# A window of three loads in flight in front of an attention and token-mixing kernel

## Chip, cores, metric

The kernel runs on one core of one Trainium2 chip. The metric is the device time of one execution in microseconds. A run counts as slow when it is more than 1.5% above the fastest of the same kernel in its rounds. Ratios below are the mean time of one kernel's fast runs over that of the other's fast runs of the same rounds, so they are not quite the ratios of the medians quoted beside them. The span in a profile is about 2 us shorter than the time of the same run. The profiled run of before (145.63 us) counts as slow.

## The reference, cut to what matters

```python
# q, k, v: (8 batches, 8 heads, 576 rows, 64), float32
scores = q_c @ k_c^T / 8        # inside chunks of 64 rows
attn   = softmax(scores);  x = attn @ v          # then x as (8, 576, 512)
W      = (x @ w_q) @ (x @ w_k)^T / 8
out    = relu(W @ x) @ w_out                     # (8, 576, 512), float32
```

For each batch 3.5 MB of q, k and v (float32) have to come in. The kernel casts them to float16 on the way, so the same batch is 1728 KB in the kernel's memory.

## The kernel before

GpSimd issues every load. One batch is 12 loads: q and k for two groups of heads, each in two parts (128 and 160 KB as float16), and v in four parts (144 KB). With the weights and batch 0, which is cut a little differently, there are 99 loads.

```python
    def load_qk(b, lo, hi):
        # ... the tiles of the batch, from a pool with three buffers
        for ti in range(2):
            for hg in range(NHG):
                nc.gpsimd.dma_start(
                    qk_in[b][ti][:, hg, lo:hi, :], qk_rows[ti][b, hg][:, lo:hi, :]
                )

    def load_v(b):
        # ...
        for o in range(2):
            for r in range(2):
                nc.gpsimd.dma_start(
                    v_bufs[b % NVB][ds(o * CH + r * 32, 32), :, 0:D], src[o, r]
                )
        # ... after the last batch: issue the stores that were held back
# ...
    load_qk(0, 0, 2 * UG); make_identity(nc, ident[:]); load_v(0)
    load_qk(0, 2 * UG, NG * UG); load_w()
    load_qk(1, 0, 4); load_qk(1, 4, NG * UG); load_v(1); load_wout()
    load_qk(2, 0, 4); load_qk(2, 4, NG * UG); load_v(2)
# ... then a fixed list of work units; when a batch's last attention unit is placed:
            load_qk(int(b) + NVB, 0, 4)
            load_qk(int(b) + NVB, 4, NG * UG)
            load_v(int(b) + NVB)
```

(The calls of the middle part are joined into fewer lines here.) GpSimd issues its loads in the order of the program. The landings of the loads are counted on eight semaphores that are used in turn (in the trace, the load of number n has the semaphore of load n-8). So load n already waits for the landing of load n-8: of the 26 idle stretches of over 0.1 us before a load, 25 end within 0.4 us after that landing. The kernel before has a window of eight.

The softmax here doesn't subtract the row's maximum and nothing guards it: scores larger than these inputs give would overflow.

## Time and profile before

| | before |
|---|---|
| time, median | 146.57 us (144.94 to 147.46), later rounds 145.75 to 146.2 us |
| profiled span | 143.6 us |
| first load issued, last load landed | 1.26 us, 99.7 us |
| mean distance between load issues | 0.94 us |
| TensorE busy, 60 to 95 us | 33.04 of 35 us |

The slices of the page of before, 40 of 3.6 us each: a digit is a busy share in tenths; GB/s is what the DMA engines moved.

```profile
PE   5998887759696788999997989999989799999700
DMA  2999999999999999999999999999999130155670
GB/s 20 137 158 144 150 142 156 152 188 179 168 149 173 164 151 176 150 154 175 172 148 173 164 147 159 168 152 363 398 366 331 42 143 8 79 216 212 258 242 18
```

Until about 97 us the loads run, at 137 to 188 GB/s; the faster slices after them are the stores. The timeline of GpSimd in before, from 66 to 72 us (start, duration, engine, line, operation; in brackets the idle time before it and what ended it):

```profile
65.62 0.86 POOL L145 DMA_DIRECT2D in_1117<-in_k_dram  x1 [0.32 <-DMA v_84<-in_v_dram]
67.11 0.86 POOL L145 DMA_DIRECT2D in_1117<-in_k_dram  x1 [0.63 <-DMA v_84<-in_v_dram]
67.97 3.25 POOL L155 DMA_DIRECT2D v_85<-in_v_dram  x4
71.21 1.52 POOL L145 DMA_DIRECT2D in_1455<-in_q_dram  x2
```

Issuing one load takes GpSimd 0.8 us; what idle time there is ends with the landing of a load eight ahead. The DMA issues of before, with the size of one and the median from issue to landing:

```profile
v_84<-in_v_dram POOLq DMA_DIRECT2D x12, 144.0 KB, 6.3
in_1116<-in_q_dram POOLq DMA_DIRECT2D x2, 160.0 KB, 6.4
```

So before keeps about seven loads in flight (6.64 us in the mean from issue to landing, over 0.94 us). The chain of waits of before, three pieces of it:

```profile
7.70 7.00 DMA v_83<-in_v_dram
...
23.06 7.43 DMA v_84<-in_v_dram
...
30.54 0.38 PE ps L227 x18
```

TensorE starts on the attention of batch 1 at 30.54 us, right after its v landed at 30.49 us. Up to there the loads set the pace. Later they run ahead: the v of batches 3 to 7 landed 6 to 11 us before its first use. The windows of before (busy time per engine with the number of instructions in brackets, granted clock, DMA share, GB/s):

```profile
core 0: us, PE busy (x) PEld busy (x) DVE busy (x) ACT busy (x) POOL busy (x), PEclk, DMA share, GB/s
60.00:95.00 35.00, 33.04 (x735) 20.40 (x732) 25.27 (x45) 24.01 (x34) 30.25 (x39) 1.00 2.25 161
```

TensorE is the busiest engine there, at 94%.

### The profile page before, as it was taken

How to read it: one execution, taken by the hardware profiler on the slowest of the kernel's cores; microseconds unless marked ns; L12 is line 12 of the kernel's file. 1: busy time of each engine (PE TensorE's matmuls, PEld its weight loads, DVE VectorE, ACT ScalarE, POOL GpSimd, SP SyncE). 2: the span in 40 equal slices, each digit the busy share in tenths (PEclk: the TensorE clock that was granted, in tenths of full speed). 3: DMA queues.
4: the chain of work that ended last, by engine and by line, in shares of the span. 5: the costliest groups of instructions: out<-in, count | busy, mean ns of one | idle time of the engine just before them, and what ended most of it. 6: DMA issues, size and time to landing. Idle time of an engine off the chain costs nothing.

```text
span 143.6 us, 5282 instructions
## 1 busy us (share of the span) xinstructions
PE 120.3 (84%) x2351; PEld 72.2 (50%) x2351; DVE 79.1 (55%) x145; ACT 71.4 (50%) x103; POOL 97.0 (68%) x137
## 2 busy tenths in 40 slices
PE   5998887759696788999997989999989799999700
PEld 2363355535384357548645755645866474444200
DVE  1000291535836678499468757876977587364100
ACT  3019047440654252728876767475485197454400
POOL 7998899858877986997996996984345010121580
PEclk9999999995999999999999999999999999999975
DMA  2999999999999999999999999999999130155670
GB/s 20 137 158 144 150 142 156 152 188 179 168 149 173 164 151 176 150 154 175 172 148 173 164 147 159 168 152 363 398 366 331 42 143 8 79 216 212 258 242 18
DMA packets 79686, 24.58 MB, mean 171 GB/s; under 512 B 76848, under 2 KB 77360, under 8 KB 79664
## 3 DMA queue, kind: packets, MB, share of 16 engines
q0 software_dynamic: 79664, 24.26, 157.7%
q8 instruction: 18, 0.29, 0.9%
q14 instruction: 4, 0.03, 0.1%
HBM read 29.62 MB, written 9.44 MB: 272 GB/s over the span
## 4 chain that ended last, share of the span: by engine, by line
PE 57%; POOL 12%; DMA 10%; DVE 9%; issue 7%; ACT 1%; POOLq 0%; DVEq 0%; ACTq 0%
PE ps L361 20%; PE ps L291 7%; PE ps L185 7%; PE ps L248 6%; DMA v_84<-in_v_dram 5%; DMA v_83<-in_v_dram 5%; PE ps L227 5%; PE ps L263 5%; PE ps L200 3%; PE ps L321 3%; DVE qk L105 3%; POOL out_dram L351 3%; DVE x_nat L236 3%; POOL in_123 L145 2%; POOL in_122 L145 2%
## 5 line engine op out<-in xcount | busy, mean ns | idle before, releaser
L351 POOL DMA_DIRECT2D out_dram<-osb x32 | 16.6, 522 | 28.7 <-ACT osb L103 15.9
L236 DVE TENSOR_TENSOR x_nat<-ps,rec 128x640 f16<-128x640 f32 x32 | 26.4, 825 | 1.1
L208 ACT ACTIVATE est<-ps 128x768 f16<-128x768 f32 x24 | 19.0, 814 | 14.5 <-PE ps L200 14.3
L105 DVE COPY qk<-ps 128x1536 f16<-128x1536 f16 x14 | 13.0, 954 | 22.7 <-PE ps L185 22.2
L103 ACT COPY osb<-ps 128x512 f32<-128x512 f32 (+1 forms) x19 | 12.9, 678 | 21.5 <-PE ps L361 18.2
L103 ACT COPY qk<-ps 128x1536 f16<-128x1536 f16 x10 | 14.3, 1440 | 11.5 <-PE ps L185 10.6
L361 PE MATMUL ps<-wout_92,rmx_88 128*128 128x512 f16 x64 | 15.2, 380 | 1.0 <-DVE rmx_88 L111 0.8
L361 PE MATMUL ps<-wout_92,rmx_89 128*128 128x512 f16 x64 | 14.8, 380 | 0.0
L422 PE MATMUL ps<-zeros 128*128 128x512 f16 x47 | 13.3, 426 | 1.7 <-DVE zeros L401 1.7
L227 PEld LDWEIGHTS <-est 64*64 64x64 f16 x640 | 8.2, 108 | 11.0 <-issue 6.3
L235 DVE RECIPROCAL rec<-ps 128x10 f32<-128x10 f32 x32 | 6.9, 215 | 11.4 <-PE ps L227 11.2
L248 PE MATMUL ps<-ident,x_nat 128*128 128x128 f16 x160 | 11.9, 225 | 0.9 <-DVE x_nat L236 0.9
L105 DVE COPY osb<-ps 128x512 f32<-128x512 f32 x13 | 8.9, 688 | 6.3 <-PE ps L361 5.8
L200 PE MATMUL ps<-qk 64*64 64x64 f16 x576 | 9.4, 196 | 2.8 <-issue 1.6
L248 PEld LDWEIGHTS <-x_nat 128*128 128x128 f16 x160 | 9.8, 101 | 3.0 <-DVE x_nat L236 1.4
L103 ACT COPY xt<-ps 128x1152 f16<-128x1152 f16 x7 | 7.9, 1122 | 6.8 <-PE ps L248 6.8
L291 PE MATMUL ps<-x_nat,wn 128*128 128x512 f16 x40 | 10.9, 406 | 0.3 <-DVE wn L105 0.2
L200 PEld LDWEIGHTS <-qk 64*64 64x64 f16 x576 | 6.7, 108 | 8.5 <-issue 4.5
L263 PE MATMUL ps<-xt,wqk_91 128*128 128x256 f16 x64 | 9.4, 287 | 0.8 <-DVE qk L105 0.4
L155 POOL DMA_DIRECT2D v_84<-in_v_dram x12 | 9.9, 841 | 0.0
L155 POOL DMA_DIRECT2D v_83<-in_v_dram x12 | 9.7, 822 | 0.0
L361 PEld LDWEIGHTS <-rmx_88 128*128 128x128 f16 x64 | 5.8, 97 | 7.5 <-DVE rmx_88 L111 1.0
(96 smaller groups left out, 205.4 us busy)
## 6 DMA issues: line engine op xcount, KB each, us to landing
out_dram<-osb POOLq DMA_DIRECT2D x16, 512.0 KB, 5.0
v_83<-in_v_dram POOLq DMA_DIRECT2D x12, 144.0 KB, 6.5
v_84<-in_v_dram POOLq DMA_DIRECT2D x12, 144.0 KB, 6.3
v_85<-in_v_dram POOLq DMA_DIRECT2D x8, 144.0 KB, 7.0
out_dram<-osb POOLq DMA_DIRECT2D x16, 64.0 KB, 2.9
wout_92<-in_moe_w_out_dram POOLq DMA_DIRECT2D x1, 512.0 KB, 8.5
in_102<-in_q_dram POOLq DMA_DIRECT2D x2, 192.0 KB, 4.1
in_103<-in_k_dram POOLq DMA_DIRECT2D x2, 192.0 KB, 5.3
```

The lines of the kernel that those rows point to most:

```text
L103: nc.scalar.copy(out_ap, in_ap)
L105: nc.vector.tensor_copy(out_ap, in_ap)
L155: nc.gpsimd.dma_start(v_bufs[b % NVB][ds(o * CH + r * 32, 32), :, 0:D], src[o, r])
L200: nc.tensor.matmul(sp[ds(CH * (xl % 2), CH), hg, ts(xl // 2, CH)], lhsT=qk[rows, 1, ts(xl, CH)], rhs=qk[rows, 0, ts(xl, CH)], start=True, ...
L208: nc.scalar.activation(e[:], sp[:, :, 0 : XG // 2 * CH], AF.Exp, scale=scale_attn)
L227: nc.tensor.matmul(xs[ds(CH * (c % 2), CH), h, j, 0 : D + 1], lhsT=est[b, g][rows, hg, ts(xl // 2, CH)], rhs=v_bufs[b % NVB][rows, hg * (N ...
L236: nc.vector.tensor_tensor(out=x_nat[b].rearrange("p j (i h d) -> p i h j d", i=NDC, h=2)[:, i], in0=xs[:, :, :, 0:D], in1=rec[:, :, :, Non ...
L248: nc.tensor.transpose(tx[:, n, ts(j, P)], x_nat[b][:, j, ts(half + 2 * n, P)], ident[:],)
L263: nc.tensor.matmul(wp[:, s, 0:nc_], lhsT=wqk16[:, i, ds(s * DH, P)], rhs=x_t[b, i % 2][:, i // 2, ds(c0, nc_)], start=(n == 0), stop=(n == ...
L291: nc.tensor.matmul(gp[:, 0, :], lhsT=w_nat[b][:, j].rearrange("p t d -> p (t d)"), rhs=x_nat[b][:, j, :], start=(j == 0), stop=(j == NJ - 1),)
L351: nc.gpsimd.dma_start(dst, src)
L361: nc.tensor.matmul(op[:, r, :], lhsT=rmx[:, i, ts((b % 2 * NU + u) * 2 + r, P)], rhs=wout16[:, i, :], start=(i == 0), stop=(i == NDC - 1),)
```

## The change

The intent: a load is issued only when the third load ahead of it has landed, so that the DMA rings hold little. GpSimd reads one element of that third load (a copy of one element), which makes GpSimd wait for its landing; then it issues the next.

```diff
+    LAG = 3
+    landed = const.tile([P, 1], F16, name="landed")
+    flying = []
+
+    def load_tile(dst, src):
+        if len(flying) >= LAG:
+            nc.gpsimd.tensor_copy(landed[0:1, :], flying[-LAG])
+        nc.gpsimd.dma_start(dst, src)
+        probe = dst[0:1]
+        while len(probe.shape) > 2:
+            probe = probe[:, 0]
+        flying.append(probe[:, 0:1])
...
-                nc.gpsimd.dma_start(
+                load_tile(
                     qk_in[b][ti][:, hg, lo:hi, :], qk_rows[ti][b, hg][:, lo:hi, :]
                 )
... (the same in load_v, load_w and load_wout)
```

It adds 96 copies. It moves no instruction of the other engines.

More of the change, by code (lines that the diff above doesn't have):

```diff
@@ L154, in load_v @@
             for r in range(2):
-                nc.gpsimd.dma_start(
+                load_tile(
                     v_bufs[b % NVB][ds(o * CH + r * 32, 32), :, 0:D], src[o, r]
@@ L164, in load_w @@
         for i, w in enumerate((moe_w_q, moe_w_k)):
-            nc.gpsimd.dma_start(
+            load_tile(
                 wqk16[:, :, ts(i, DH)], w.rearrange("(i p) j -> p i j", p=P)
@@ L169, in load_wout @@
     def load_wout():
-        nc.gpsimd.dma_start(wout16[:], moe_w_out.rearrange("(i p) m -> p i m", p=P))
+        load_tile(wout16[:], moe_w_out.rearrange("(i p) m -> p i m", p=P))
     qk_t, est, x_nat, x_t, w_nat, g_sb, o_sb = {}, {}, {}, {}, {}, {}, {}
```

## The prediction

> **What bounds the kernel now.** All 99 loads are issued by GpSimd, one after another, from 1.26 to 93.4 us (timeline of GpSimd); the last lands at 99.7 us. During that time the DMA row of the 40 slices stands at 9 almost everywhere and moves about 155 GB/s, so the load stream runs at the pace of the DMA engines: 12 loads (one batch, 1.73 MB) take 11.45 us, 0.95 us a load. GpSimd needs only 0.75 to 0.9 us to issue one; its waits name landings of earlier loads, because eight completion semaphores are used in turn. So today's window is eight: at most issues six or seven loads are in flight, and a load takes 5 to 8 us from issue to landing.
>
> TensorE is busy 94% from 60 to 95 us (windows). Loads gate it only early: the chain of waits runs through v of batch 0 (7.0 us of DMA, to 14.70) and v of batch 1 (7.4 us, landing 30.49, first use 30.54); v of batch 2 has 0.4 us to spare (44.49, 44.87). Later batches arrive ahead of use: q and k of batches 3 to 7 by about 5 to 10 us, v by 6, 7, 9, 11 and 11 us.
>
> **What the change does.** It adds 96 one-element copies on GpSimd and shrinks the window from eight to three. The copies themselves are cheap (estimate 0.1 to 0.2 us, from the 0.1 us memsets and the 0.27 us identity memset). The round trip is not: a slot is reused only after issue + descriptor generation + transfer + completion + wake-up. The first load (192 KB, alone in flight) landed 3.53 us after issue; the last 64 KB store 1.86 us. Taking off generation (1.00, 0.50) and transfer (about 1.3, 0.17), both leave about 1.2 us fixed. The Trainium skill, "DMA: Bandwidth & Descriptors", section "Anatomy of one DMA", puts the fixed cost at about 2.0 us, generation included; the trace agrees (1.7 to 2.2). So a 128 to 160 KB load with little ahead of it needs 0.85 + 1.2 + 1.0 = 3.05 us; landing to issue costs 0.28 us today, with the copy 0.4 to 0.5. Loop 3.5 us / 3 = 1.15 us a load, against 0.95: DMA no longer saturated, a batch takes 13.3 to 14.2 us instead of 11.45 (estimate).
>
> **Critical path.** The first q, k and v of batch 0 land about 0.5 us sooner; then loads fall behind: batch 1 delays TensorE by 1.5 to 3 us. Then 2 to 2.5 us a batch are lost against the slack of 5 to 11 us, which is eaten around batch 4 or 5; from there TensorE waits at each transpose of q and k. Last landing 112 to 118 us instead of 99.7. Replaying the TensorE uses of before against such landings shifts the end by 4 to 12 us; centre 8.5. Stores follow the last load, long before TensorE ends.
>
> Predicted 155 us, 8 in 10 between 148.5 and 164. Faster by 2%: 3%; within 2%: 17%; slower: 80%.
>
> **Signs.** Right: issue to landing falls to 3 to 4 us; DMA digits of 7 and 8, about 125 GB/s; GpSimd waits on the load three ahead at nearly every copy; issues 1.1 to 1.2 us apart, the last near 112 us; TensorE stalls on in and v after 60 us. Wrong: issues 1.0 us apart or less, last landing before 106 us, time within 2%.
>
> **What would make it wrong.** If packets flow faster with fewer loads in flight (the lone first load reached 178 GB/s), three would nearly saturate and the slack would hide the rest. If the copy's semaphore round trip costs 0.7 us or more, each load takes 1.3 us and the time passes 160.

## The result

| | before | after |
|---|---|---|
| time, median | 145.75 us (144.48 to 147.46, 4 runs) | 194.38 us (192.62 to 195.1, 4 runs) |
| ratio | | 1.3357 (1.3184 to 1.353) |
| profiled span | 143.6 us | 192.1 us |
| distance between load issues | 0.94 us | 1.54 us |
| last load landed | 99.7 us | 156.3 us |
| TensorE's mean granted clock | 0.970 | 0.857 |

The slices of after, each now 4.8 us:

```profile
PE   6985791758639765995599169938993899999930
PEclk9999797587975995799669958996998599999996
DMA  5998989999999999999999999999999999955571
GB/s 52 121 103 78 77 81 114 94 88 135 99 107 106 93 94 111 85 105 105 94 98 92 106 108 74 105 113 98 81 97 93 100 288 384 388 189 220 218 278 50
```

The DMA digits are 9 as before, but the engines move 96 GB/s instead of 160 (mean from 20 us to just before the last landing). The packets of one engine overlap: the page's part on queues puts their times at 157.7% of the 16 engines' span in before and 106.6% in after. The digit stops at 9, so it can't tell a full stream from a thinner one; the line of GB/s can. The granted clock of TensorE (row PEclk) falls after the slices in which it waits: slice by slice the digits of PE and PEclk hardly go together (correlation 0.15), but those of PEclk do with those of PE one slice earlier (0.88).

The timeline of GpSimd in after, the same stretch as above:

```profile
66.97 0.18 POOL L140 COPY landed<-in_478 1x1 f16<-1x1 f16 x1 [1.13 <-DMA in_478<-in_q_dram]
67.42 0.84 POOL L141 DMA_DIRECT2D in_478<-in_q_dram  x1 [0.28 <-issue]
68.67 0.18 POOL L140 COPY landed<-in_479 1x1 f16<-1x1 f16 x1 [0.41 <-DMA in_479<-in_k_dram]
69.13 0.87 POOL L141 DMA_DIRECT2D in_478<-in_q_dram  x1 [0.28 <-issue]
70.00 0.18 POOL L140 COPY landed<-in_479 1x1 f16<-1x1 f16 x1
70.12 0.86 POOL L141 DMA_DIRECT2D in_479<-in_k_dram  x1
71.03 0.18 POOL L140 COPY landed<-in_478 1x1 f16<-1x1 f16 x1
71.47 0.86 POOL L141 DMA_DIRECT2D in_479<-in_k_dram  x1 [0.27 <-issue]
```

A copy takes 0.18 us, and where it had to wait, another 0.28 us pass before the load is issued. The same DMA issues:

```profile
v_84<-in_v_dram POOLq DMA_DIRECT2D x12, 144.0 KB, 4.0
in_1177<-in_q_dram POOLq DMA_DIRECT2D x2, 160.0 KB, 4.0
```

A load lands sooner than before (4.0 us, not 6.3 us), yet fewer land in a microsecond. The chain of waits of before, as shares of the span by engine:

```profile
PE 57%; POOL 12%; DMA 10%; DVE 9%; issue 7%; ACT 1%; POOLq 0%; DVEq 0%; ACTq 0%
```

And of after, where the DMA has taken the place of TensorE:

```profile
DMA 60%; PE 15%; POOL 10%; issue 10%; DVE 1%; POOLq 1%; ACT 0%; ACTq 0%; DVEq 0%
```

One link of that chain in after (start, duration, what):

```profile
64.04 4.51 DMA in_479<-in_k_dram
68.59 0.08 issue
68.67 0.18 POOL landed L140
68.85 0.28 issue
69.13 3.40 DMA in_478<-in_q_dram
```

Landing (at 68.55 us), 0.58 us of handing over (a piece of 0.04 us is too short for this view), then the next load: the chain is a slot of the window that goes round. TensorE hangs on it, as its timeline in after shows (three waits from this window):

```profile
89.73 0.24 PE L200 MATMUL ps<-ident,in_834 128*64 128x128 f16 x1 [1.17 <-DMA in_834<-in_q_dram]
90.86 0.41 PE L200 MATMUL ps<-ident,in_834 128*64 128x128 f16 x7 [0.88 <-DMA in_834<-in_q_dram]
...
92.52 0.24 PE L200 MATMUL ps<-ident,in_835 128*64 128x128 f16 x1 [1.15 <-DMA in_835<-in_k_dram]
```

And the windows of after, for the stretch shown of before:

```profile
60.00:95.00 35.00, 25.52 (x514) 16.60 (x512) 17.75 (x32) 10.95 (x17) 22.64 (x47) 0.84 1.19 99
```

TensorE gets through 514 matmuls in these 35 us instead of 735. After 60 us its waits of over 0.1 us that end with the landing of a load are 19 in after, 21.5 us together, and none in before.

### The profile page after: what moved, and what is told of

Read it like the earlier page. It is cut to its first block, busy times and chain, and to the rows that moved or that the text cites. A ratio compares the mean times of both kernels' runs of the same rounds, so it can differ in the third digit from the quotient of the medians.

```text
span 192.1 us, 5454 instructions
## 1 busy us (share of the span) xinstructions
PE 140.6 (73%) x2351; PEld 84.0 (44%) x2351; DVE 80.0 (42%) x145; ACT 71.5 (37%) x103; POOL 113.0 (59%) x233
## 2 busy tenths in 40 slices
DMA packets 79688, 24.60 MB, mean 128 GB/s; under 512 B 76848, under 2 KB 77360, under 8 KB 79664
## 3 DMA queue, kind: packets, MB, share of 16 engines
q0 software_dynamic: 79664, 24.26, 106.6%
## 4 chain that ended last, share of the span: by engine, by line
DMA 60%; PE 15%; POOL 10%; issue 10%; DVE 1%; POOLq 1%; ACT 0%; ACTq 0%; DVEq 0%
DMA v_83<-in_v_dram 8%; DMA v_85<-in_v_dram 7%; DMA v_84<-in_v_dram 7%; PE ps L376 6%; DMA in_162<-in_q_dram 5%; DMA in_103<-in_q_dram 5%; DMA in_1905<-in_k_dram 5%; DMA in_134<-in_q_dram 4%; DMA in_834<-in_q_dram 4%; POOL landed L140 3%; DMA in_479<-in_k_dram 2%; PE ps L278 2%; DMA in_1177<-in_q_dram 2%; DMA in_163<-in_k_dram 2%; POOL out_dram L366 2%
## 5 line engine op out<-in xcount | busy, mean ns | idle before, releaser
L376 PE MATMUL ps<-wout_92,rmx_89 128*128 128x512 f16 x64 | 17.4, 428 | 0.0
L437 PE MATMUL ps<-zeros 128*128 128x512 f16 x47 | 15.0, 468 | 1.7 <-DVE zeros L416 1.7
L376 PE MATMUL ps<-wout_92,rmx_88 128*128 128x512 f16 x64 | 15.2, 380 | 1.3 <-DVE rmx_88 L111 0.8
L263 PE MATMUL ps<-ident,x_nat 128*128 128x128 f16 x160 | 12.6, 234 | 0.3 <-DVE x_nat L251 0.2
L242 PEld LDWEIGHTS <-est 64*64 64x64 f16 x640 | 8.7, 117 | 8.7 <-issue 3.9
L109 ACT ACTIVATE rmx_88<-ps 128x512 f16<-128x512 f32 (+1 forms) x15 | 6.2, 473 | 15.9 <-PE ps L336 15.9
L278 PE MATMUL ps<-xt,wqk_91 128*128 128x256 f16 x64 | 11.3, 327 | 0.3 <-DVE xt L105 0.2
L263 PEld LDWEIGHTS <-x_nat 128*128 128x128 f16 x160 | 10.4, 105 | 2.2 <-DVE x_nat L251 0.9
L376 PEld LDWEIGHTS <-rmx_89 128*128 128x128 f16 x64 | 6.4, 107 | 8.8 <-issue 3.8
L215 PEld LDWEIGHTS <-qk 64*64 64x64 f16 x576 | 7.3, 120 | 6.5 <-issue 3.5
```

Of the source, the lines that this page charges most:

```text
L242: nc.tensor.matmul(xs[ds(CH * (c % 2), CH), h, j, 0 : D + 1], lhsT=est[b, g][rows, hg, ts(xl // 2, CH)], rhs=v_bufs[b % NVB][rows, hg * (N ...
L263: nc.tensor.transpose(tx[:, n, ts(j, P)], x_nat[b][:, j, ts(half + 2 * n, P)], ident[:],)
L278: nc.tensor.matmul(wp[:, s, 0:nc_], lhsT=wqk16[:, i, ds(s * DH, P)], rhs=x_t[b, i % 2][:, i // 2, ds(c0, nc_)], start=(n == 0), stop=(n == ...
L376: nc.tensor.matmul(op[:, r, :], lhsT=rmx[:, i, ts((b % 2 * NU + u) * 2 + r, P)], rhs=wout16[:, i, :], start=(i == 0), stop=(i == NDC - 1),)
L437: nc.tensor.matmul(wp[:, 0, :], lhsT=zeros[:, 0:P], rhs=zeros[:], start=True, stop=True)
```

## The experiments

The theory after the result: a slot of the window is used again after one round, which is issue to landing plus landing to the next issue; with W slots a load is issued every round / W. The prediction had put the round at 3.5 us; in after it was 3.96 + 0.66 = 4.62 us, and 4.62 / 3 = 1.54 us is the distance that was measured. That the two agree is bookkeeping: measured so, the two parts of a round always add up to W distances. What can be wrong is which part sets the round, and that is what the runs below test. Rivals: the copies themselves are the cost; or the DMA engines are slow in some way that doesn't depend on the window. The means below are over each load after the first four. For the parts of a load I assigned the packet records of the trace to the loads in order of issue, by size and number; where only one load is in flight this is exact.

### The copies without the window

```diff
-            nc.gpsimd.tensor_copy(landed[0:1, :], flying[-LAG])
+            nc.gpsimd.tensor_copy(landed[0:1, :], still[0:1, :])   # still: set once at the start
```

> The same 96 one-element copies, each just ahead of a load, but they read a tile that no load writes, so they wait for nothing and the window stays eight. Theory (the narrow window costs the time, the copies are only handoffs): GpSimd needs about 0.98 us a load (generation plus copy), the stream is paced as before at 0.94 to 1.0 us, last landing 100 to 104 us, time 145 to 150 us. Rival (96 more GpSimd instructions between loads are the cost): a load every 1.3 us or more, time above 170 us.

Measured: 146.92 us median (143.41 to 147.82) against 146.2 us, a load every 0.963 us, last landing 101.3 us; only one run was fast, so there was no ratio.

> The same kernel as copies_alone, which had too few fast runs for a ratio. Theory: 96 copies that wait for nothing cost at most 0.02 us a load on the DMA-bound stream (0.963 against 0.940 us), hidden by the slack: same, ratio 1.00 to 1.02.

Measured: 146.01 us median against 146.01 us, ratio 1.0025 (0.9843 to 1.0207). The interval reaches just past 2%, so the verdict is formally unclear, but 96 copies that wait for nothing are worth no more than 3 us of the 48. The rival of the copies as work falls; what they cost as a handover is the next run.

### The window without the copies

```diff
-        if len(flying) >= LAG:
-            nc.gpsimd.tensor_copy(landed[0:1, :], flying[-LAG])
-        nc.gpsimd.dma_start(dst, src)
+        this = nc.gpsimd.dma_start(dst, src)
+        if len(flying) >= LAG:
+            # a dependence: this load waits for the landing of the third ahead
+            tc.add_manual_dep(this.ins, flying[-LAG].ins.name, ...)
+        flying.append(this)
```

> Window of three without the copy: the load itself waits for the landing of the third load ahead. Theory: in the changed kernel the loop of one slot was 4.0 us issue to landing plus 0.66 us landing to next issue; the second falls to about 0.3 us, loop 4.3 us, 1.43 us a load, last landing 145 us, time 180 to 186 us. Rival (the copy and its semaphore round trip are the main cost): time falls below 160 us.

Measured: 186.54 us median (182.6 to 191.59, two of four runs slow), ratio 1.2732 (1.2308 to 1.3155); the profiled span is 180.8 us. Issue to landing 3.90 us, landing to issue 0.40 us in the mean (median 0.29 us), a load every 1.44 us, last landing 146.1 us. As expected: taking the copy away returns 0.26 us of landing to issue, and the ratio goes from 1.336 to 1.273, about a fifth of the loss; the window keeps the rest. One link of the chain of waits in this run, to hold against the one of after:

```profile
57.91 3.68 DMA in<-in_q_dram
61.59 0.28 issue
61.87 3.54 DMA in<-in_q_dram
```

### A window of one: what a load costs alone

```diff
-    LAG = 3
+    LAG = 1
```

> A window of one: each load is alone in flight, so its issue to landing is the latency without any queueing, per size. Prediction's value: 3.05 us for 128 to 160 KB. Theory now: the lone latency is about 3.0 us for 128 KB, 3.3 us for 160 KB and 3.5 us for the 144 KB of v (mean 3.3), the rest of the 4.0 us seen with three is queueing behind the other two and behind instruction fetches; 3.3 + 0.6 = 3.9 us a load, last landing about 390 us, time about 425 us. Rival (no queueing with three, the lone latency is 4.0 us): 4.6 us a load, time about 490 us.

Measured: 433.26 us (one run), a load every 4.00 us, 3.39 + 0.61 us a round, last landing 397.5 us. The DMA issues of this run:

```profile
v<-in_v_dram POOLq DMA_DIRECT2D x32, 144.0 KB, 3.6
in<-in_q_dram POOLq DMA_DIRECT2D x14, 160.0 KB, 3.4
in<-in_q_dram POOLq DMA_DIRECT2D x14, 128.0 KB, 3.1
```

A load that is quite alone takes 3.1 to 3.6 us, not the 3.05 us of the prediction. Its parts, in the mean: 0.81 us generation, 0.70 us to the first packet, 1.53 us from first to last packet, 0.35 us from the last packet to the landing. The transfer is the surprise: the prediction had about 1.0 us.

### Windows of two, four, five and six

The edit is LAG = 2, 4, 5, 6.

> Window of two. The window of one measured 3.39 us from issue to landing and 0.61 us from landing to the next issue; three in flight 3.98 and 0.66. Theory (latency of a lone load plus a little queueing): 3.6 + 0.62 = 4.2 us for two, 2.1 us a load, last landing about 211 us, time about 249 us. Rival (the DMA engines are a bottleneck of their own at about 100 GB/s whatever the window, which is what the three showed): 1.6 us a load, time about 200 us.

> Window of four. Theory (rate = window over round trip, more loads overlapping in the engines, queueing growing a little): 4.3 + 0.65 us over 4 = 1.24 us a load, about 124 GB/s, last landing about 127 us, time about 165 us. Rival of the prediction (round trip 3.5 us): 0.95 us a load, time 146 to 148 us. Rival (engines limited to about 100 GB/s): time stays above 185 us.

> Window of five. Theory: 4.8 + 0.7 us over 5 = 1.1 us a load, last landing about 112 us, time 149 to 154 us, slower than before by 2 to 5%.

> Window of six. Theory: the window no longer limits; GpSimd with generation plus copy needs 0.98 us a load and the DMA engines 0.94: 1.0 us a load, last landing about 103 us, inside the slack of later batches, time within 2% of before (145 to 149 us).

Measured, with the other windows beside them. GB/s is from 20 us to just before the last landing, without the instruction fetches; "slow" marks a profiled run of that state.

| window | us a load | issue to landing | landing to issue | GB/s | last landing | span | time, median | ratio |
|---|---|---|---|---|---|---|---|---|
| 1 | 4.00 | 3.39 | 0.61 | 37 | 397.5 | 431.5 | 433.26 (1 run) | |
| 2 | 2.06 | 3.50 | 0.61 | 72 | 206.6 | 239.5 | 241.25 (1 run) | |
| 3 (the change) | 1.54 | 3.96 | 0.66 | 96 | 156.3 | 192.1 | 194.38 | 1.336 |
| 4 | 1.28 | 4.41 | 0.75 | 117 | 131.8 | 168.2 | 170.53 | 1.177 (1.160 to 1.194) |
| 5 | 1.14 | 4.70 | 1.01 | 132 | 118.4 | 154.4 | 157.63 | 1.086 (1.071 to 1.100) |
| 6 | 1.06 | 5.16 | 1.23 | 142 | 110.2 | 151.6 (slow) | 151.83 | 1.035 (1.018 to 1.051) |
| 8, copies that wait for nothing | 0.96 | 6.13 | 1.59 | 156 | 101.3 | 145.8 (slow) | 146.92 | |
| 8, before | 0.94 | 6.64 | 0.92 | 160 | 99.7 | 143.6 (slow) | 146.57 | 1 |

In each row the two times added and divided by the window give the distance between loads, as they must. What the table shows is that issue to landing hardly grows from one load in flight to two (3.39 and 3.50 us), and from there more slowly than the window does, so that the rate rises with each load added. The rival of a fixed rate of about 100 GB/s falls: 37 to 160 GB/s, by the window alone. Windows of four and five came out slower than expected (165 and 149 to 154 us), and six missed the expected tie by a ratio of 1.035: with more loads in flight a slot also waits until GpSimd, which issues in order, is free, and I had not allowed enough for that. The record's verdict for the windows of four, five and six is "unclear" (so it is for the window without the copies and for the larger loads with a window of three), but each interval lies above 1, and all but that of six above 1.02. No window came out faster than before, so there was no better version to try.

### Larger loads in a window of three, and one of them alone

```diff
-            load_qk(int(b) + NVB, 0, 4)
-            load_qk(int(b) + NVB, 4, NG * UG)
+            load_qk(int(b) + NVB, 0, NG * UG)      # likewise for batches 1 and 2
```

> Window of three with copies as in the change, but q and k of one batch and head group come as one 288 KB load from batch 1 on instead of 128 + 160 KB, so a batch has 8 loads and the window holds up to twice the bytes. Theory (a load's time in its slot is mostly fixed, little of it grows with bytes): the slot loop of a merged load is about 5.2 us, of v 4.6 us, so a batch takes about 13.5 us instead of 18.6 us; last landing 115 to 122 us, time 150 to 158 us. Rival (what is slow is the transfer itself with few loads in flight, so time goes with bytes): a batch still takes 17 us or more, time above 180 us.

Measured: 168.82 us median (167.88 to 170.62), ratio 1.1658 (1.1426 to 1.189). A batch takes 15.2 us (mean of the last five, from landing to landing), against 18.6 us in after and 11.0 us in before. A merged load takes 5.94 us from issue to landing, not 4.6. That is between theory and rival, so my "mostly fixed" was too strong: bytes count too. Hence the next run, the same with a window of one.

> Window of one with 288 KB loads: each alone. From the lone loads of 96, 128 and 160 KB (first to last packet 1.06, 1.37, 1.57 us) the transfer of one load grows by about 0.032 us for each of its packets per engine, so 72 packets take about 2.6 us and issue to landing is about 4.6 us, 5.2 us a merged load; the rival, a fixed part that dominates, gives 3.9 us. The lone rate is then about 110 GB/s within a load, against 160 GB/s of before with seven in flight.

Measured (one run, 369.03 us): 4.72 us from issue to landing for 288 KB, close to the 4.6 us expected. Two lines of its DMA issues:

```profile
v<-in_v_dram POOLq DMA_DIRECT2D x32, 144.0 KB, 3.7
in<-in_q_dram POOLq DMA_DIRECT2D x14, 288.0 KB, 4.7
```

Against 3.13 us for 128 KB, 160 KB more cost 1.59 us (0.24 us of it in generation): a lone load moves at 103 GB/s (163,840 bytes / 1.59 us, bytes as they land in float16), and about 1.9 us of it don't grow with bytes (3.13 - 1.27). In the packet records a lone load has 19 packets in flight in the mean over the 16 engines while any is in flight, little more than one an engine; before has 34. A packet of 256 B lasts 42 ns alone, so 16 engines with one each would move about 97 GB/s (estimate), close to the lone rate. The window of three is no better off in this respect: 19 packets in flight, since the packets of a load take 1.55 us from first to last and a load comes every 1.54 us, so that the loads in flight hardly overlap in this part. What keeps an engine from taking more packets of a lone load is not shown by any run.

### The loads without the computation

The list of work units is emptied, all loads are issued in the same order, and zeros are stored at the end: the result is wrong.

> Wrong result on purpose: the 99 loads of the changed kernel with their copies and window of three, in the same order, and no computation (zeros are stored at the end), so no engine competes and there are few instructions to fetch. With one load in flight the latency was 3.39 us, with two 3.50, with three 3.96. Theory (about half of the rise is that loads in flight are delayed by 16 KB instruction fetches on a DMA engine: loads that met one took 4.26 us, the others 3.70): latency about 3.7 us, 1.43 us a load, last landing about 144 us. Rival (the rise is the three loads queueing on one another in the DMA engines): 3.9 to 4.0 us, 1.52 us or more a load, last landing 152 us or later.

> Wrong result on purpose: the same without computation for the kernel before, window of eight through its semaphores. If the 0.94 us a load of before is the DMA engines' own pace, it stays at 0.90 to 0.95 us and the last load lands at 95 to 100 us; if computation slowed it, it falls towards the 0.8 us that GpSimd needs to issue one, last landing about 85 us.

Measured with the window of three: 3.78 us from issue to landing, 1.47 us a load, last landing 149.6 us. With the window of eight: 0.92 us a load, last landing 98.4 us, 162 GB/s. The slices of the former:

```profile
GB/s 44 136 102 81 76 92 108 104 103 134 59 122 111 90 97 101 117 91 104 97 115 88 96 103 119 91 103 105 106 90 94 104 113 97 322 424 426 422 420 201
```

So it isn't computation that imposes the 0.94 us a load of before. That it is the DMA engines' own pace is not shown: these loads too have a window of eight, GpSimd is busy 0.82 us of the 0.92 with issuing, and no run has a wider window. With the window of three the latency is 0.39 us above the lone 3.39 us even when nothing else runs: the loads hold one another up. Another 0.18 us appears with the computation. Instruction fetches are a likely part of it: in after, 15 packets of 16 KB each (and four of 8 KB), about 1 us long, came by during the loads, the 44 loads that were in flight when one began took 4.26 us and the other 51 took 3.70 us, and this run has hardly any fetches (two of 8 KB during the loads). Those 51 were no slower than the loads of this run (3.78 us), so the fetches can account for all of the 0.18 us; with the window of one, where no other load is in the way, the loads beside a fetch were slower too (3.75 us for 16 of them, 3.32 us for the others). Still, this run removed the computation along with the fetches, so no run changed the fetches alone. The result lies between the two expectations.

## Why the prediction was wrong

**Right: direction and mechanism.** The window shrank from eight to three, the DMA stream lost its overlap, and TensorE came to wait for q and k in every batch after 60 us. Issue to landing fell to 3.96 us, the upper edge of the 3 to 4 us foretold. The copies are cheap (0.18 us each, as predicted 0.1 to 0.2).

**Right: the critical path.** I moved each TensorE use of a load in the trace of before to the landings of another run plus the shift so far. For the landings of after this gives 48.3 us; the span grew by 48.5 us. For windows of 1, 2, 4 and 5 it gives 286.5, 95.7, 24.0 and 11.6 us; the spans grew by 287.9, 95.9, 24.6 and 10.8 us. A recount of this replay agrees to about 1 us; for the window of six, whose profile is a slow one, it gives about 4 us where the span grew by 8.0. So the slack and its use were understood; with the right landings the replay would have been right. It also leaves no room for the rival that TensorE's lower granted clock (0.857, not 0.970) made the loss: the landings alone give it, and without any computation the window of three still lands its last load at 149.6 us.

**Wrong: the size of the round.** The step that failed is "a 128 to 160 KB load with little ahead of it needs 0.85 + 1.2 + 1.0 = 3.05 us; landing to issue ... with the copy 0.4 to 0.5. Loop 3.5 us / 3 = 1.15 us a load". Measured against it:

| term | predicted | alone (window 1) | three in flight (after) |
|---|---|---|---|
| generation | 0.85 | 0.81 | 0.81 |
| fixed (to the first packet, and from the last to the landing) | 1.2 | 1.05 | 1.60 |
| transfer, first to last packet | 1.0 | 1.53 | 1.55 |
| landing to next issue | 0.45 | 0.61 | 0.66 |
| round | 3.5 | 4.00 | 4.62 |

- The transfer was the largest error within one load. I had scaled it from the rate of before, where some seven loads overlap (160 GB/s), and from the first load (178 GB/s). But 178 GB/s was its best half microsecond (3.5 to 4.0 us), and it was not alone: the next two loads were issued 1.00 and 1.83 us after it, before it landed. The same load quite alone, in the run with a window of one, took 1.67 us from first to last packet, 118 GB/s; larger against smaller loads alone give 103 GB/s.
- The handover, where GpSimd was free and waiting, is 0.12 us from landing to copy, 0.18 us of copy and 0.28 us to the issue; I had counted today's 0.28 us once and most of the copy.
- Three loads in flight still queue: 0.57 us above the lone latency. I had assumed none ("with little ahead of it"). It sits in the waits before the first packet and after the last.

Together 1.1 us a round, 0.39 us a load. Over 98 distances this is 38 us of last landing (156.3 instead of 118), and once the slack is gone all of it reaches the end. The small errors were multiplied by 98; that is also why the range of 148.5 to 164 was too narrow. Of the two dangers that the prediction named, a slow handover came near (0.66 us; it had said 0.7), and alone it would have made 3.05 + 0.66 = 3.71 us a round, 1.24 us a load; the other, packets that flow faster with fewer loads, was the opposite of what happened.

**Wrong: two signs.** "DMA digits of 7 and 8": they stayed at 9 while the rate fell by 40%. The predicted rate of 125 GB/s would have been that of a window of four to five. "GpSimd waits on the load three ahead at nearly every copy": at only 50 of the 96 copies did it wait for more than 0.1 us after it was free.

**The Trainium skill.** "DMA: Bandwidth & Descriptors", section "Anatomy of one DMA", puts a DMA at about 2.0 us plus its bytes over 436 GB/s. The fixed part agrees: 1.9 us by the two lone sizes. The slope doesn't: an estimate by that formula for 288 KB is 2.7 us (3.4 us if the 576 KB of float32 that are read are counted); measured: 4.72 us. The same page warns, in its section "Specifications", that transfers under 512 B don't run at line rate; nearly all packets here are of 128 or 256 B (76,848 of 79,686 in before are under 512 B). The lone loads of the window of one point the same way: from first to last packet 88 GB/s for v in packets of 128 B, 105 GB/s for 160 KB of q or k in packets of 256 B, 150 GB/s for the one load of w_out, 512 KB in packets of 1 KB. But these differ in more than the packet, and no run changed the packet alone. The measured slope decides.

## What to carry to other kernels

The number of loads in flight is a resource: the rate of a load stream is window over round trip until something saturates, and here, with loads of about 150 KB, it still rose from a window of six (142 GB/s) to one of eight (160 GB/s). Before narrowing a window, measure the round trip with one load in flight (a window of one is an easy run), including the handover, and don't take the transfer time of a lone load from the rate of an overlapped stream. A load that lands sooner is no gain when fewer of them land per microsecond, and a stream of many loads multiplies an error in one of them by their number.

## What the Trainium skill lacked or had wrong

- "DMA: Bandwidth & Descriptors", "Anatomy of one DMA": the slope of bytes / 436 GB/s doesn't hold for the casting loads, in packets of 256 B. Alone, 128 KB took 3.13 us and 288 KB 4.72 us: 103 GB/s.
- The same page doesn't say how the rate depends on how many DMAs are in flight from one issuing engine: 37, 72, 96, 117, 132, 142 and 160 GB/s with windows of 1, 2, 3, 4, 5, 6 and 8.
- No page gives what a load loses when an instruction fetch (here a packet of 16 KB, about 1 us long) runs beside it: in after, loads beside one took 4.26 us and others 3.70 us; with a window of one 3.75 and 3.32 us.
- "GPSIMD Engine Reference" has no figure for a one-element copy and for a DMA issue behind a wait: 0.18 us for the copy, and 0.28 us from it to the issue where it had waited; 0.28 us from landing to issue where the load waits itself.
